# Moving a kernel's stores to another engine's queue, re-anchoring its early loads and shifting one tile in the order

## The chip, the cores and the metric

The kernel runs on one core of one Trainium2 chip. The metric is the device time of one execution in microseconds, as the median of several executions. Before the change it was 1954.47 us (three runs, 1954.44 to 1956.24). One us is 0.05% of the whole.

## The reference

The kernel computes a block and all its gradients: a layer norm, a branch A (a shift convolution over four steps, then a long convolution through an FFT) and a branch B (an MLP with a ReLU gate).

```python
def _A_ref(q, k, v, shift_k, ssm_k, ssm_D):        # S = 2048, D = 1024
    k_shift = sum(k_pad[:, t:t + S, :] * shift_k[:, ks - 1 - t] for t in range(4))
    kv = k_shift * v
    y = irfft2(rfft2(pad(kv)) * rfft2(pad(ssm_k)))[:S] + kv * ssm_D
    return q * y
def _B_ref(x, W_gate, W_up, W_down):               # F = 3584
    gate = x @ W_gate
    return (relu(gate) * (x @ W_up)) @ W_down
xn  = layernorm(x)
out = x + _A_ref(xn, k, v, ...) + _B_ref(xn, ...)
# returned: out and, by jax.vjp, the gradients of all inputs      [abridged]
```

## The kernel before

TensorE works through the MLP in blocks of 512 hidden columns. The A branch is a generator: it handles 128 channels (a *group*) at a time, eight groups in all, and its small matmuls are dealt out between the MLP's. Each engine works through its instructions in the order in which the program was built: a scheduler places each instruction by its priority and by the time at which it expects its inputs.

Loads and nearly all stores go out from SyncE, in one queue:

```python
    def load(self, out, in_):                       # A branch
        self.pri.now()
        ins = self.nc.sync.dma_start(out=out, in_=in_)
        if self.pin:
            self.tc.keep_in_program_order(ins)

    def store(self, out, in_):                      # A branch
        self.pri.late()
        self.nc.sync.dma_start(out=out, in_=in_)
```

The pieces of one group that the argument needs (the group's order of steps, cut):

```python
    def h_tile(self, st):                           # the filter tile
        hT = self.ttile("hT")
        pst = self.ps.tile([P, 16, P], BF16, name="pst", tag="aps")   # PSUM, 2 buffers for the A branch
        for r in range(16):
            self.nc.tensor.transpose(pst[:, r, :], hv[:, r, :], self.identA[:])
        self.vcopy(hT[:, 0:16, :], pst[:])          # VectorE; frees the PSUM buffer
        return hT

    def steps(self):
        self.shift_rows()                           # ends in the store of sk_d
        self.pin = True
        nx = self.loads_1(0)                        # hn, gt, xt, sD
        self.loads_2(nx)                            # kp, vt, skb
        self.pin = False
        hT = self.h_tile(nx)
        for gi in range(self.NG):
            ...
            self.taps(st, ksh, kp, ...)             # 4 products and 3 sums on VectorE, 128 x 2048
            self.tt(kvt[:, 0:16, :], ksh[:], vt[:], ALU.mult)
            ...                                     # nx = loads_1(gi + 1)
            gks = self.gradients(st, gkv, ksh)      # stores gv
            self.store_time(self.y_d, cg, yt)
            self.grad_k(st, gks)                    # stores gk
            self.loads_2(nx)
            ...
            hT = self.h_tile(nx)                    # next group's filter
            yield from self.inv_b_chan(Ch, ghn, 2000)   # two groups of matmuls, ps5, each into an A PSUM buffer
            self.store(self.out_gh[cg, :], ghf)
```

In a group, `gv`, `y`, `gk`, `gt`, `xt`, `kp` and `vt` move between a [2048, 1024] matrix and [128, 16, 128] tiles, in halves of 1024 rows of 256 bytes. The MLP stores `h_d` and `ug_d` for the weight gradients later, and its weights are loaded two blocks deep: `wg`, `wu` as plain loads and `wdT` as four DMA transposes. The early loads are tied to a store:

```python
                        stored = nc.sync.dma_start(out=h_d[...], in_=ht[:])
                        self.stored = stored
    ...
                        with self.tc.issue_after(self.stored.ins):
                            load(5 + sp // 2)                       # layer-norm input
    ...
                        with self.tc.issue_after(self.stored.ins):
                            first = self.weights(Wg, Wu, Wd, fb + 1)
```

Of the kernel before, what the change touches and what calls it, by code (L numbers as in the profile page):

```python
# [17 lines left out]
P = 128  # L18
# [24 lines left out]
class ABranch:  # L43
# [41 lines left out]

    def store(self, out, in_):
        self.pri.late()
        self.nc.sync.dma_start(out=out, in_=in_)

    def open(self):  # L90
        R = "right"
# [333 lines left out]
    def steps(self):  # L425
# [4 lines left out]
        nx = self.loads_1(0)  # L430
        self.loads_2(nx)
        self.pin = False
        hT = self.h_tile(nx)
        for gi in range(self.NG):
            st, nx = nx, None
# [94 lines left out]
class LnMlp:  # L530
# [126 lines left out]

    def load_T(self, src, st, name):
        t = self.act_tile(name)
        self.nc.sync.dma_start_transpose(out=t[:].rearrange("p (a b) -> p a b", b=P),  # L660
                                         in_=src[st * P:(st + 1) * P, :])
        return t

    def flip_xn(self, st):
# [7 lines left out]
    def hidden(self, first, goT, load, ln, tables, Wg, Wu, Wd, g, xn_d, h_d, ug_d):  # L672

        nc, HS = self.nc, self.ST // 2
        for half in range(2):
            s0 = half * HS
# [3 lines left out]
            for fb in range(self.FB):  # L680
                self.pri.now()
                cols = slice(fb * 512, fb * 512 + 512)
                wg, wu, wd = first or self.weights(Wg, Wu, Wd, fb)
                first = None
                ru, ahead = {}, fb + half == 0
# [7 lines left out]
                def gate_up(sp):  # L693
                    flip(sp + 2)
                    for s in (sp, sp + 1):
                        ru[s] = self.e2_tile("ru")
                        ps = self.ps_tile("ps_g")
                        self.gemm8(ps, xT[s], wg)
                        nc.scalar.activation(out=ru[s][:, 0, :], in_=ps[:], func=ACT.Relu)
                        yield 1730  # L700
                        self.pri.now()
                    for s in (sp, sp + 1):
                        ps = self.ps_tile("ps_u")
                        self.gemm8(ps, xT[s], wu)
                        ht = self.e1_tile("ht")
                        nc.vector.scalar_tensor_tensor(out=ru[s][:, 1, :], in0=ru[s][:, 0, :], scalar=0.0, in1=ps[:],  # L706
                                                       op0=ALU.is_gt, op1=ALU.mult)
                        nc.vector.tensor_tensor(out=ht[:], in0=ru[s][:, 0, :], in1=ru[s][:, 1, :], op=ALU.mult)
                        stored = nc.sync.dma_start(out=h_d[(s0 + s) * P:(s0 + s + 1) * P, cols], in_=ht[:])
                        self.stored = stored  # L710
                        yield 1730
                        self.pri.now()

                def grad(sp):
                    for s in (sp, sp + 1):
                        if ahead and s == sp + 1:
                            flip(min(sp + 6, HS))
                        ps = self.ps_tile("ps_h")
                        self.gemm8(ps, gT[s], wd)
                        gh = self.e1_tile("gh")  # L720
                        nc.scalar.copy(out=gh[:], in_=ps[:])  # L721
                        nc.vector.tensor_tensor(out=ru[s][:], in0=ru[s][:], in1=gh[:].rearrange(
                            "p (o f) -> p o f", o=1).to_broadcast([P, 2, 512]), op=ALU.mult)
                        nc.sync.dma_start(out=ug_d[(s0 + s) * P:(s0 + s + 1) * P, :, cols], in_=ru[s][:])
                        yield 1730
                        self.pri.now()

# [7 lines left out]
                for sp in range(0, HS, 2):  # L735
                    self.pri.now()
                    while len(gT) < min(sp + (6 if ahead else 2), HS):
                        gT.append(self.load_T(g, s0 + len(gT), "goT"))
                    if not ahead:
                        yield from gate_up(sp)  # L740
                    yield from grad(sp)
                    if ahead and sp + 4 < HS:
                        with self.tc.issue_after(self.stored.ins):
                            load(5 + sp // 2)
                        yield from gate_up(sp + 4)
                        next(ln)
                    if ahead and sp == 0:
                        with self.tc.issue_after(self.stored.ins):
                            first = self.weights(Wg, Wu, Wd, fb + 1)
                if ahead:  # L750
                    with self.tc.issue_after(self.ln_act.ins), self.tc.issue_after(self.ln_dve.ins):
# [27 lines left out]
    def grad_down(self, g, h_d, out_wd):  # L779
        nc = self.nc  # L780
        self.pri.now()
        gn = self.nat_tiles(g, "g_nat")
        for fb in range(self.FB):
            self.pri.now()
            hs = self.slab(h_d, fb, "hs")
            if fb == 0:
                self.pri.now()
                ps = [self.ps_tile("ps_d") for _ in range(4)]
                wo = [self.e2_tile("wo") for _ in range(2)]
# [9 lines left out]
                        yield 1730  # L799
                        self.pri.now()  # L800
                for j in range(2):
                    nc.sync.dma_start(out=out_wd[j * P:(j + 1) * P, :], in_=wo[j][:].rearrange("p a f -> p (a f)"))
            for j in range(2 if fb == 0 else 0, 4):
                self.pri.now()
                wo = self.e2_tile("wo")
# [3 lines left out]
                                           lambda st: gn[st][:, ob * 512:ob * 512 + 512])  # L809
                    nc.scalar.copy(out=wo[:, ob, :], in_=ps[:])  # L810
                f0 = fb * 512 + j * P
                nc.sync.dma_start(out=out_wd[f0:f0 + P, :], in_=wo[:].rearrange("p a f -> p (a f)"))

    def grad_in(self, xn_d, ug_d, out_wg, out_wu):
        nc = self.nc
# [2 lines left out]
        for fb in range(self.FB):  # L818
            for w, out in ((1, out_wg), (0, out_wu)):
                self.pri.now()  # L820
                sl = self.slab(ug_d[:, w, :], fb, "ugs")
                for dp in range(self.DT // 2):
                    self.pri.now()
                    wo = self.e2_tile("wi")
                    for d in range(2):
# [1 line left out]
                        ps = self.ps_tile("ps_w")  # L827
                        yield from self.gemm16(ps, lambda st: xn[st][:, dc * P:(dc + 1) * P], sl)
                        nc.scalar.copy(out=wo[:, d, :], in_=ps[:])  # L829
                    nc.sync.dma_start(out=out[dp * 256:dp * 256 + 256, fb * 512:fb * 512 + 512].rearrange(  # L830
                        "(s p) f -> p s f", p=P), in_=wo[:])

    def open_right(self, Wd):
# [209 lines left out]
```

## Time and profile before

| | before |
|---|---|
| median of the runs | 1954.5 us |
| TensorE busy, of the profiled span of 1957.4 us | 1915.1 us |
| TensorE idle | 42.3 us, 12.5 of it the first layer norm |
| mean granted TensorE clock (1 is full speed) | 0.995 |
| VectorE waiting for gv stores | 15.9 us |

The profiled run itself took 1959.14 us, more than any of the timed ones. The view of TensorE's waits names, for each group of its instructions, what ended the idle time before it: engine and line of the waiting instruction, "<-", the releaser, then us in total, times, longest. The prediction below shows it whole, with the queue of SyncE.

### The profile page before, as it was taken

The numbers are of one execution on the slowest core, as the hardware profiler recorded it, in microseconds if no ns is written. First come the engines' busy times: TensorE is split into PE (matmuls) and PEld (weight loads), VectorE is DVE, ScalarE is ACT, GpSimd is POOL, SyncE is SP. The second block draws the span as 40 slices with busy tenths as digits, with TensorE's granted clock in tenths as the row PEclk, the third lists the DMA queues.
The fourth block names the chain that finished last, engine by engine and source line by source line (L and its number), as shares of the span: only waits on it lengthen the run. The fifth ranks groups of instructions, "written<-read, shape, count | busy, mean of one in ns | idle before, by whom it ended". The sixth has DMA issues, their size and how long they took to land.

```text
span 1957.4 us, 36111 instructions
## 1 busy us (share of the span) xinstructions
PE 1915.1 (98%) x15502; PEld 882.0 (45%) x15502; DVE 914.1 (47%) x1374; ACT 616.8 (32%) x852; POOL 14.7 (1%) x37
## 2 busy tenths in 40 slices
PE   7899999999999999999999999999999999999998
PEld 3434444444444444444444444444444444444443
DVE  6677677577678557355255435300222222222222
ACT  6544354444444425444344354311000000000000
POOL 1000000000000000000000000000000000000000
PEclk9999999999999999999999999999999999999999
DMA  9975766984674774462763542691999954545441
GB/s 255 237 157 163 178 179 174 207 202 136 168 193 130 202 213 136 113 185 78 224 158 119 127 135 85 159 324 39 239 255 235 210 135 121 123 120 124 123 121 38
DMA packets 615970, 319.08 MB, mean 163 GB/s; under 512 B 450937, under 2 KB 585089, under 8 KB 615809
## 3 DMA queue, kind: packets, MB, share of 16 engines
q1 hardware_dynamic: 605312, 295.79, 60.2%
q10 hardware_dynamic: 9216, 16.78, 2.8%
q0 software_dynamic: 1280, 4.20, 0.8%
q8 instruction: 121, 1.98, 0.4%
q14 instruction: 41, 0.33, 0.1%
HBM read 141.56 MB, written 95.44 MB: 121 GB/s over the span
## 4 chain that ended last, share of the span: by engine, by line
PE 90%; DVE 4%; DMA 3%; issue 2%; ACT 1%; SPq 0%; POOL 0%; DVEq 0%; ACTq 0%; POOLq 0%
PE ps_w L774 20%; PE ps_x L908 19%; PE ps_o L874 10%; PE ps_g L643 9%; PE ps_u L643 9%; PE ps_d L774 8%; PE ps_h L643 8%; PE ps L66 6%; DMA ln_x<-in_A_q_dram 1%; PE ps_d L794 1%; DVE flp L304 1%; ACT ln_j L597 1%; DMA kp<-in_A_k_dram 1%; DVE gk L74 0%; DVE ru L706 0%
## 5 line engine op out<-in xcount | busy, mean ns | idle before, releaser
L774 PE MATMUL ps_w<-ugs,xn_nat 128*128 128x512 bf16 x1792 | 399.4, 379 | 2.1 <-DMA xn_nat<-xn_d 1.3
L643 PEld LDWEIGHTS <-xnT 128*128 128x128 bf16 x1792 | 172.2, 99 | 218.3 <-issue 19.6
L774 PEld LDWEIGHTS <-xn_nat 128*128 128x128 bf16 x1792 | 170.3, 98 | 208.6 <-issue 5.9
L643 PE MATMUL ps_u<-wu,xnT 128*128 128x512 bf16 x896 | 209.4, 384 | 4.7 <-DMA wu<-in_B_W_up_dram 4.1
L643 PE MATMUL ps_g<-wg,xnT 128*128 128x512 bf16 x896 | 209.0, 383 | 2.2 <-DVE xnT L669 2.2
L643 PE MATMUL ps_h<-wdT,goT 128*128 128x512 bf16 x896 | 206.7, 379 | 0.6 <-DMA wdT<-in_B_W_down_dram 0.6
L921 ACT ACTIVATE w<-xn,m 128x512 f32<-128x512 bf16 x32 | 24.3, 806 | 559.5 <-issue 317.2
L908 PE MATMUL ps_x<-wgT,ggT 128*128 128x512 bf16 x896 | 198.6, 379 | 0.0
L908 PE MATMUL ps_x<-wuT,guT 128*128 128x512 bf16 x896 | 198.6, 379 | 0.0
L874 PE MATMUL ps_o<-wd,hT 128*128 128x512 bf16 x896 | 193.6, 379 | 0.0
L774 PE MATMUL ps_d<-g_nat,hs 128*128 128x512 bf16 x832 | 187.4, 379 | 0.0
L304 DVE STREAM_TRANSPOSE flp<-C 128x1024 f32<-128x1024 f32 x48 | 90.4, 1934 | 102.8 <-ACT C L70 102.8
L829 ACT CAST wi<-ps_w 128x512 bf16<-128x512 f32 x112 | 65.6, 587 | 222.4 <-PE ps_w L774 207.9
L908 PEld LDWEIGHTS <-ggT 128*128 128x128 bf16 x896 | 87.7, 98 | 105.7
L908 PEld LDWEIGHTS <-guT 128*128 128x128 bf16 x896 | 87.7, 98 | 105.7
L874 PEld LDWEIGHTS <-hT 128*128 128x128 bf16 x896 | 87.7, 98 | 105.7
L643 PEld LDWEIGHTS <-goT 128*128 128x128 bf16 x896 | 85.1, 98 | 103.5 <-issue 4.5
L304 DVE STREAM_TRANSPOSE flp<-B 128x1024 f32<-128x1024 f32 x48 | 90.4, 1940 | 83.3 <-ACT B L70 83.2
L910 DVE CUSTOM_DVE_ANT_0 gx<-ps_x,gy 128x512 f32<-128x512 f32 x32 | 22.1, 691 | 216.5 <-PE ps_x L908 216.5
L774 PEld LDWEIGHTS <-hs 128*128 128x128 bf16 x832 | 78.5, 98 | 95.5 <-issue 4.3
L721 ACT CAST gh<-ps_h 128x512 bf16<-128x512 f32 x112 | 65.2, 585 | 165.7 <-PE ps_h L643 153.7
L867 DVE TENSOR_TENSOR ya<-ya,xe 128x1024 bf16<-128x1024 bf16 x16 | 11.1, 692 | 226.9 <-DMA xe<-xn_d 226.9
(165 smaller groups left out, 1541.6 us busy)
## 6 DMA issues: line engine op xcount, KB each, us to landing
ug_d<-ru SPq DMA_DIRECT2D x112, 256.0 KB, 3.5
ugs<-ug_d SPq DMA_DIRECT2D x112, 256.0 KB, 4.6
wg<-in_B_W_gate_dram SPq DMA_DIRECT2D x56, 256.0 KB, 4.2
wu<-in_B_W_up_dram SPq DMA_DIRECT2D x56, 256.0 KB, 3.4
h_d<-ht SPq DMA_DIRECT2D x112, 128.0 KB, 2.4
hs<-h_d SPq DMA_DIRECT2D x56, 256.0 KB, 4.7
out_dram<-wi SPq DMA_DIRECT2D x56, 256.0 KB, 3.1
gt<-in_grad_out_dram SPq DMA_DIRECT2D x32, 256.0 KB, 3.4
```

The source lines that it names most:

```text
L66: self.nc.tensor.matmul(out, lhsT=lhsT, rhs=rhs, start=start, stop=stop)
L304: self.nc.vector.transpose(out=df[:, c0:c0 + 32, :], in_=sf[:, c0:c0 + 32, :])
L597: total = nc.scalar.activation(out=jk[:], in_=xt[:, j, :], func=ACT.Copy, accum_out=sm[:, 0, j:j + 1])
L643: self.nc.tensor.matmul(ps[:], lhsT=xT[:, kt * P:(kt + 1) * P], rhs=w(kt), start=(kt == 0), stop=(kt == self.DT - 1))
L721: nc.scalar.copy(out=gh[:], in_=ps[:])
L774: self.nc.tensor.matmul(ps[:], lhsT=lhsT(st), rhs=rhs(st), start=(st == 0), stop=(st == self.ST - 1))
L794: nc.tensor.matmul(ps[i][:], lhsT=hs(st)[:, j * P:(j + 1) * P], rhs=gn[st][:, ob * 512:ob * 512 + 512], start=(st == 0), stop=(st == self. ...
L829: nc.scalar.copy(out=wo[:, d, :], in_=ps[:])
L874: nc.tensor.matmul(ps[:], lhsT=hT[:, kt, :], rhs=self.wd[:, kt, oc], start=(kt == 0), stop=(kt == self.FT - 1))
L908: nc.tensor.matmul(ps[:], lhsT=T[:, kt, :], rhs=W[:, kt, oc], start=(i == 0), stop=(i == n - 1))
L910: V.tensor_tensor_reduce(out=gx[:, oc], in0=ps[:], in1=gy[:, oc], scale=1.0, scalar=0.0, op0=ALU.add, op1=ALU.add, accum_out=m[:, ob:ob + 1])
L921: nc.scalar.activation(out=w[:, oc], in_=xn[:, oc], func=ACT.Identity, scale=m[:, 5:6], bias=m[:, 4:5])
```

## The change

The intent: SyncE's queue is in order, and loads stand in it behind stores that wait for VectorE. All stores up to the weight gradients move to GpSimd, so that SyncE holds loads only in that part; the early loads are anchored on a transpose load instead of a store; and the first filter tile is made some steps later than its load.

```diff
     def store(self, out, in_):
         self.pri.late()
-        self.nc.sync.dma_start(out=out, in_=in_)
+        self.nc.gpsimd.dma_start(out=out, in_=in_)
@@ steps
         self.pin = False
+        yield 8000
         hT = self.h_tile(nx)
@@ load_T
-        self.nc.sync.dma_start_transpose(out=..., in_=src[st * P:(st + 1) * P, :])
+        self.loaded = self.nc.sync.dma_start_transpose(out=..., in_=src[st * P:(st + 1) * P, :])
@@ hidden
-                        stored = nc.sync.dma_start(out=h_d[...], in_=ht[:])
-                        self.stored = stored
+                        nc.gpsimd.dma_start(out=h_d[...], in_=ht[:])
@@ hidden
-                        nc.sync.dma_start(out=ug_d[...], in_=ru[s][:])
+                        nc.gpsimd.dma_start(out=ug_d[...], in_=ru[s][:])
@@ hidden, twice
-                        with self.tc.issue_after(self.stored.ins):
+                        with self.tc.issue_after(self.loaded.ins):
@@ weight gradients, three places (out_wd twice; out_wg and out_wu)
-                nc.sync.dma_start(out=out_wd[...], in_=wo...)
+                nc.gpsimd.dma_start(out=out_wd[...], in_=wo...)
```

(Index expressions are cut.)

More of the change, by code (lines that the diff above doesn't have):

```diff
@@ L659, in load_T @@
         t = self.act_tile(name)
-        self.nc.sync.dma_start_transpose(out=t[:].rearrange("p (a b) -> p a b", b=P),
-                                         in_=src[st * P:(st + 1) * P, :])
+        self.loaded = self.nc.sync.dma_start_transpose(out=t[:].rearrange("p (a b) -> p a b", b=P),
+                                                       in_=src[st * P:(st + 1) * P, :])
         return t
@@ L708, in gate_up @@
                         nc.vector.tensor_tensor(out=ht[:], in0=ru[s][:, 0, :], in1=ru[s][:, 1, :], op=ALU.mult)
-                        stored = nc.sync.dma_start(out=h_d[(s0 + s) * P:(s0 + s + 1) * P, cols], in_=ht[:])
-                        self.stored = stored
+                        nc.gpsimd.dma_start(out=h_d[(s0 + s) * P:(s0 + s + 1) * P, cols], in_=ht[:])
                         yield 1730
@@ L723, in grad @@
                             "p (o f) -> p o f", o=1).to_broadcast([P, 2, 512]), op=ALU.mult)
-                        nc.sync.dma_start(out=ug_d[(s0 + s) * P:(s0 + s + 1) * P, :, cols], in_=ru[s][:])
+                        nc.gpsimd.dma_start(out=ug_d[(s0 + s) * P:(s0 + s + 1) * P, :, cols], in_=ru[s][:])
                         yield 1730
@@ L747, in hidden @@
                     if ahead and sp == 0:
-                        with self.tc.issue_after(self.stored.ins):
+                        with self.tc.issue_after(self.loaded.ins):
                             first = self.weights(Wg, Wu, Wd, fb + 1)
@@ L801, in grad_down @@
                 for j in range(2):
-                    nc.sync.dma_start(out=out_wd[j * P:(j + 1) * P, :], in_=wo[j][:].rearrange("p a f -> p (a f)"))
+                    nc.gpsimd.dma_start(out=out_wd[j * P:(j + 1) * P, :], in_=wo[j][:].rearrange("p a f -> p (a f)"))
             for j in range(2 if fb == 0 else 0, 4):
@@ L811, in grad_down @@
                 f0 = fb * 512 + j * P
-                nc.sync.dma_start(out=out_wd[f0:f0 + P, :], in_=wo[:].rearrange("p a f -> p (a f)"))
+                nc.gpsimd.dma_start(out=out_wd[f0:f0 + P, :], in_=wo[:].rearrange("p a f -> p (a f)"))
     def grad_in(self, xn_d, ug_d, out_wg, out_wu):
@@ L829, in grad_in @@
                         nc.scalar.copy(out=wo[:, d, :], in_=ps[:])
-                    nc.sync.dma_start(out=out[dp * 256:dp * 256 + 256, fb * 512:fb * 512 + 512].rearrange(
+                    nc.gpsimd.dma_start(out=out[dp * 256:dp * 256 + 256, fb * 512:fb * 512 + 512].rearrange(
                         "(s p) f -> p s f", p=P), in_=wo[:])
```

## The prediction

> **What bounds the kernel now.** I read the engine summary first, then who TensorE waited for, then the clock by slices of 5 us, then the queue that issues the transfers. The page opens with:
>
> ```profile
> PE 1915.1 (98%) x15502; PEld 882.0 (45%) x15502; DVE 914.1 (47%) x1374; ACT 616.8 (32%) x852; POOL 14.7 (1%) x37
> ```
>
> TensorE (PE) is busy for 1915.1 of 1957.4 us. The change touches no matmul, so all that it can win is the 42.3 us in which PE is idle, plus time that PE spends at a reduced clock. The view of PE's waits over the whole span splits the idle time (columns: engine, line, what ended the wait, us in total, times, longest):
>
> ```profile
> PE pst_x L667 <- DVE ln_b L609: 10.4, 1, 10.4
> PE ps L66 <- DVE hT L78: 6.1, 4, 2.5
> PE pst L293 <- DMA hn<-in_A_ssm_k_dram: 4.5, 1, 4.5
> PE ps_u L643 <- DMA wu<-in_B_W_up_dram: 4.1, 1, 4.1
> PE ps_g L643 <- DVE xnT L669: 2.2, 2, 1.1
> PE pst_x L667 <- DVE ln_x L624: 2.1, 1, 2.1
> PE ps L66 <- DVE flp L304: 1.7, 3, 0.9
> PE ps_w L774 <- DMA xn_nat<-xn_d: 1.3, 3, 0.7
> PE ps_w L774 <- DMA out_dram<-wo: 0.7, 1, 0.7
> PE ps_h L643 <- DMA wdT<-in_B_W_down_dram: 0.6, 1, 0.6
> PE ps_u L643 <- ACT gh L721: 0.5, 1, 0.5
> ```
>
> The eleven lines sum to 34.2 us. The first and the sixth (12.5 us) are the first layer norm, before PE has anything to do; the rest of the 42.3 us, 8.1, is mostly the drain after the last matmul. That leaves 34.2 - 12.5 = 21.7 us of waits which the order of transfers could touch, and only two of them are loads of some size: hn, the first filter tile, 4.5, and wu, a block of the up weights, 4.1. After 960 us the view shows no wait of PE.
>
> The slices of 5 us show what each pause costs afterwards (columns: stretch, its length, busy time of PE, PEld, DVE, ACT and POOL with instruction counts, granted clock, DMA share, GB/s):
>
> ```profile
> 90.00:95.00 5.00, 0.76 (x8) 0.77 (x9) 0.95 (x2) 0.00 (x0) 0.00 (x0) 0.82 1.16 227
> 95.00:100.00 5.00, 5.00 (x21) 2.43 (x20) 1.22 (x1) 0.00 (x0) 0.00 (x0) 0.50 1.35 166
> 125.00:130.00 5.00, 3.34 (x9) 1.21 (x9) 4.90 (x5) 0.00 (x0) 0.00 (x0) 0.73 1.11 238
> ```
>
> After the hn wait the clock is 0.50 for a whole slice, after the wu wait 0.73. At (1 - clock) x 5 us these are 0.9 + 2.5 and 1.35 us, and the slice 130 to 135 (clock 0.93) adds 0.35.
>
> Why those two loads are late is in the timeline of the issuing queue (start, length, queue, line, what, how many):
>
> ```profile
> 87.94 0.56 SPq L88 DMA_DIRECT2D sk_d<-sk_t  x1
> 88.59 0.54 SPq L724 DMA_DIRECT2D ug_d<-ru  x1
> 89.19 0.60 SPq L82 DMA_DIRECT2D hn<-in_A_ssm_k_dram  x1
> ...
> 111.70 5.34 SPq L709 DMA_DIRECT2D h_d<-ht  x2
> 119.08 2.92 SPq L724 DMA_DIRECT2D ug_d<-ru  x2
> 122.09 3.01 SPq L636 DMA_DIRECT2D wu<-in_B_W_up_dram  x4
> ```
>
> The queue is in order. The hn load goes out at 89.19 behind stores of ug_d, and PE reaches it half a us later; wu goes out at 122.09 behind stores of h_d and ug_d that wait for a VectorE which is busy throughout 115 to 130 us. Both are waits behind stores, not a lack of bandwidth: the DMA share from 110 to 120 is 0.08 to 0.10.
>
> **What the Trainium skill says.** "DMA: Bandwidth & Descriptors", section "Issuing engines are not separate DMA queues", says that transfers issued from several engines share the same 16 DMA engines and that spreading them only saves issue time. I read it as: no bandwidth to win, only the wait in order; the DMA shares above agree. The same page, "Latency and other measured facts", gives about 1 us to the first byte from GpSimd against about 0.6 from SyncE. In this trace the 16 xn_d stores from GpSimd land in a median of 6.0 us and stores of the same 256 KB from SyncE in 2.1 to 4.4, though the former all fall in the crowded first 80 us. "SBUF — State Buffer", section "SBUF: two separate sides", warns that VectorE operations in its two-port modes lock GpSimd out of writing descriptors. The trace shows little of it: the xn_d issues take 539 ns at the median and 682 at most beside a VectorE that is 46% to 83% busy in those slices. "TensorE: Matmul & The Clock Gate", Part 1, puts the clock at one half after about 3.4 us of idleness, and full again after about 3.4 busy us; the 0.50 slice after a 4.5 us wait agrees.
>
> **The change part by part.** (1) 112 h_d, 112 ug_d, 28 wo and 56 wi stores, the 48 halves of gv, y and gk, 8 ghn and 3 small ones, 367 in all, move from SyncE to GpSimd. At 0.54 us (xn_d) that is 198 us of GpSimd issue time spread over 1270 us, on an engine busy 14.7 us: off the path. The 48 halves have rows of 256 bytes, 1024 of them against 128 for xn_d; if issue time scaled with rows they would cost 8 x 0.54 = 4.3 us each (estimate), together 207 instead of 26 us. The engine would still be under a third busy.
>
> (2) SyncE's rows fall from 1016 to some 650. In the order of the changed kernel hn is queued directly after the last layer-norm load, behind no store; that load went out at 49.0 us before, so hn should be in the buffer some 25 us before PE asks. xt, kp and vt follow at about 75 to 85 instead of 91.6 to 101. The wu block, the third, takes the buffers of the second block's gate tiles, whose last matmuls in the timeline run from 105.04 to 108.7. Before it SyncE's new order has only loads whose waits end sooner. So it can go out at about 109 and, at the 3.4 us of the wu issues, land at about 113, ten us before PE wants it at 122.5.
>
> (3) The 8000 ns step moves the filter transpose in PE's order. Counting matmul time at 2.4 GHz, it stands 3.5 us later (74.4 against 71.0 us of PE work), and all of the A branch follows 8 to 9 us later. It lies inside the MLP's matmuls, and 97 us of matmuls without any A work follow its end, so the shift costs nothing by itself.
>
> (4) The layer-norm and weight loads now hang on a transpose load instead of on a store: earlier, in a stretch where the DMA share is already about 1. A risk of one or two us.
>
> Sum: hn 4.5 + 0.9 + 2.5 = 7.9; wu 4.1 + 1.35 + 0.35 = 5.8; together 13.7. I keep 80%, 11, since PE arriving sooner can meet VectorE (busy 4.9 of 5 us around 125) instead. The hT waits, 6.1 us, hang on VectorE's in-order work; VectorE itself waited 15.9 us for gv stores and 7.3 for kp loads, which the change moves both ways. I take 1 us off for these. The small loads (xn_nat, wdT: 1.9) give perhaps 1, and I set 2 us against the sum for new waits. Net 11 + 1 + 1 - 2 = 11 us: 1954.5 - 11 = 1943.5.
>
> **The rivals.** *The wait is only replaced.* VectorE fell behind at 115 to 130 because tap work arrives together with MLP work. With loads earlier this work starts earlier, which speaks against it; but if PE then waits for flp, kvt or PSUM banks, the gain shrinks to 3 to 5 us: 1950.
>
> *GpSimd stores land so late that buffers bind.* The A branch has three time tiles for hT, kvt, gv, gks, yt, gk and ghn, each freed by a store. Against 4.4 us now, 10 us of landing would add 5 to 6 us to VectorE's wait in each of 8 groups. Also the zeroing of kp sits in GpSimd's queue behind stores. If a third of 8 x 6 us reached PE, +16 us would cancel the gain: 1955 to 1960. For it: 6.0 us of xn_d, and the row counts. Against: PE has other matmuls in its order between dependent A steps, and the gv stores today are themselves held up on SyncE.
>
> *More is won.* If all 21.7 us of waits and all clock loss went (mean clock 0.995, so 0.005 x 1957 = 9.8 us, 0.8 of it after the last matmul) the win would be 30.7 us, 1.6%. So over 2% (39.1 us) is out of reach unless the start also shortens, for which I see nothing.
>
> **Range and chances.** Centre 1943.5. The low end, 1934, takes both loads in full and most of hT with its clock loss; the high end, 1955, is the buffer rival cancelling everything. Faster by 2% needs below 1915.4: 1 in 100. Slower by 2% needs above 1993.6, some 50 us of new waits, only if descriptor making is far slower than xn_d shows: 3 in 100. Same: 96 in 100.
>
> **What would show it.** Right: the waits on hn and wu are absent, the clock stays at 1.00 from 85 to 135, PE's busy time falls by about 4 us and its idle time by 7 or more; the hn issue starts before 65 us; the stretch after 1369 is unchanged. Wrong: waits of PE on hT, flp or ps banks that grow beyond 10 us in sum, VectorE waiting for gv, gk or y stores well above 20 us, or GpSimd's store issues of several us each. An early wait on ln_x, were it to grow, would refute step (4).

## The result

The changed kernel takes 1971.14 us in the median (four runs, 1968.44 to 1972.56), the kernel before 1954.45 us on the same chip (four runs, 1952.49 to 1956.24). Ratios here and below are the mean time of one kernel's fast runs over that of the other's fast runs of the same rounds, so not quite the ratio of the medians: here 1.0084, 95% interval 1.0066 to 1.0101. That is 0.8% slower, the same at a threshold of 2%. The prediction said 1943.5 with a range of 1934 to 1955, so it missed, and in sign.

The engine summary of the changed kernel:

```profile
PE 1917.8 (97%) x15502; PEld 882.5 (45%) x15502; DVE 914.6 (46%) x1374; ACT 618.4 (31%) x852; POOL 255.6 (13%) x404
```

GpSimd (POOL) is at 13%, no bound. TensorE's idle time rose from 42.3 to 52.4 us of a span of 1970.2. Its waits:

```profile
PE ps L66 <- DVE hT L78: 11.5, 6, 3.0
...
PE ps_h L644 <- DMA wdT<-in_B_W_down_dram: 10.0, 6, 3.3
PE ps L66 <- DVE flp L304: 4.1, 2, 3.6
...
PE ps_w L774 <- DMA xn_nat<-xn_d: 1.9, 4, 1.3
PE ps_g L644 <- DVE ru L707: 1.9, 3, 1.3
```

Set this against the same view of before in the prediction. The waits on hn (4.5) and on wu (4.1) are gone, as predicted. In their place wdT went from 0.6 to 10.0, hT from 6.1 to 11.5, flp from 1.7 to 4.1. The wdT waits fall into two stretches, at 69 to 76 and at 415 to 422 us. The slices of 5 us (stretch, length, busy time of PE, PEld, DVE, ACT, POOL, clock, DMA share, GB/s) show the second:

```profile
415.00:420.00 5.00, 1.06 (x5) 0.29 (x4) 1.09 (x2) 1.01 (x1) 0.54 (x1) 1.00 1.19 243
420.00:425.00 5.00, 4.04 (x10) 1.28 (x10) 0.69 (x1) 0.59 (x1) 0.00 (x0) 0.51 1.09 315
425.00:430.00 5.00, 5.00 (x20) 2.11 (x19) 0.69 (x1) 2.27 (x4) 1.35 (x2) 0.80 0.19 65
```

TensorE lost 3.94 + 0.96 = 4.9 us, and the clock of 0.51 and 0.80 took 0.49 x 5 + 0.20 x 5 = 3.5 more. At 70 to 85 us the same reading gives 5.1 and, with clocks of 0.54 and 0.78, 3.4. A sum over the changes: the wdT waits with their clock, 8.4 + 8.5 = 16.9, less the 0.6 of before; hT and flp +7.8; ru and xn_nat, 1.9 + 0.6 = +2.5; hn and wu, -13.7 by the prediction's count. That is +12.9, against 12.8 between the two profiled spans (that it agrees to a tenth is chance). The profiled runs took 1971.92 and 1959.14 us; the medians lie 16.7 us apart, so some 4 us of the loss are outside this sum.

The queue of SyncE (start, length, queue, line, what, how many) ahead of the second stretch:

```profile
385.93 0.36 SPq L82 DMA_DIRECT2D skb<-sk_d  x1
397.97 0.60 SPq L82 DMA_DIRECT2D xt<-xn_d  x1
398.67 1.00 SPq L82 DMA_DIRECT2D hn<-in_A_ssm_k_dram  x1
399.76 2.56 SPq L637 DMA_DIRECT2D wu<-in_B_W_up_dram  x4
402.37 0.98 SPq L82 DMA_DIRECT2D xt<-xn_d  x1
403.45 16.07 SPq L652 DMA_TRANSPOSE wdT<-in_B_W_down_dram  x4
```

SyncE stands for 12 us, and the next in its queue is xt, whose pool is shared with VectorE's taps (e7 below tests whether that buffer is the reason). Then two halves of xt, hn and wu, 2 MB together, go out within 5.4 us, and the four wdT transposes take 16 us behind them. In the kernel before they went out one by one between stores, and wdT cost TensorE 0.6 us in the whole run:

```profile
408.32 1.26 SPq L651 DMA_TRANSPOSE wdT<-in_B_W_down_dram  x1
...
410.31 1.25 SPq L651 DMA_TRANSPOSE wdT<-in_B_W_down_dram  x1
...
412.26 2.57 SPq L651 DMA_TRANSPOSE wdT<-in_B_W_down_dram  x2
```

And one of the six hT waits, first on VectorE, then on TensorE (columns as above; in brackets the idle time before and what ended it):

```profile
242.84 2.47 DVE L74 TENSOR_TENSOR ksh<-ksh,tap 128x2048 bf16<-128x2048 bf16 x2
245.23 1.22 DVE L74 TENSOR_TENSOR tap<-kp,skb 128x2048 bf16<-128x2048 bf16 x1
246.37 1.22 DVE L78 COPY hT<-pst 128x2048 bf16<-128x2048 bf16 x1
247.50 1.21 DVE L74 TENSOR_TENSOR ksh<-ksh,tap 128x2048 bf16<-128x2048 bf16 x1
```

```profile
239.56 1.16 PE L293 MATMUL pst<-ident,hn 128*128 128x128 bf16 x16
...
242.29 0.63 PE L66 MATMUL ps<-RB,flp 128*128 128x64 bf16 x16
242.75 1.89 PE L644 MATMUL ps_u<-wu,xnT 128*128 128x512 bf16 x8
247.64 0.63 PE L66 MATMUL ps<-RB,flp 128*128 128x64 bf16 x16 [2.99 <-DVE hT L78]
```

TensorE had made pst, the transposed filter, by 240.72. VectorE copies it at 246.37, because the next group's taps (ksh, tap) stand in front of the copy. Until then pst keeps one of the A branch's two PSUM buffers, and the second ps5 group of matmuls (247.64) has nowhere to go. The order of the built program shows this for every group. Counted are the tap operations (4 products, 3 sums) of a group that stand on VectorE before the copy of that same group's hT:

```
                      group  0  1  2  3  4  5  6  7    sum
kernel before                0  1  2  3  4  5  2  3     20
changed kernel               1  6  6  6  7  6  6  6     44
```

The stores themselves, which I had feared, are not late: gv's halves land in 4.6 us instead of 4.4, y's in 4.7 instead of 4.3, gk's in 5.1 instead of 4.4 (medians of those landings that the traces show, 5 to 8 of 16 before and 9 to 14 after). They also go out sooner: between a tile being ready and its store going out lay a median of 7.3 us for gv, 14.3 for y and 13.7 for ghn before, and 0.3 to 1.1 us after (worked out from the two traces).

### The profile page after: what moved, and what is told of

Read it like the earlier page. It is cut to its first block, busy times and chain, and to the rows that moved or that the text cites. A ratio compares the mean times of both kernels' runs of the same rounds, so it can differ in the third digit from the quotient of the medians.

```text
span 1970.2 us, 36231 instructions
## 1 busy us (share of the span) xinstructions
PE 1917.8 (97%) x15502; PEld 882.5 (45%) x15502; DVE 914.6 (46%) x1374; ACT 618.4 (31%) x852; POOL 255.6 (13%) x404
## 3 DMA queue, kind: packets, MB, share of 16 engines
q0 software_dynamic: 27424, 87.07, 14.3%
## 4 chain that ended last, share of the span: by engine, by line
PE 89%; DVE 5%; issue 2%; DMA 2%; ACT 1%; SPq 0%; POOL 0%; DVEq 0%; ACTq 0%; POOLq 0%
PE ps_w L774 19%; PE ps_x L908 19%; PE ps_o L874 10%; PE ps_h L644 9%; PE ps_g L644 9%; PE ps_u L644 9%; PE ps_d L774 9%; PE ps L66 6%; DVE tap L74 1%; DVE flp L304 1%; DMA wdT<-in_B_W_down_dram 1%; DVE ksh L74 1%; DMA xn_nat<-xn_d 1%; DMA kp<-in_A_k_dram 0%; DVE gk L74 0%
## 5 line engine op out<-in xcount | busy, mean ns | idle before, releaser
L644 PE MATMUL ps_h<-wdT,goT 128*128 128x512 bf16 x896 | 211.2, 386 | 10.0 <-DMA wdT<-in_B_W_down_dram 10.0
L304 DVE STREAM_TRANSPOSE flp<-C 128x1024 f32<-128x1024 f32 x48 | 90.7, 1940 | 107.0 <-ACT C L70 107.0
L707 DVE SCALAR_TENSOR_TENSOR ru<-ru,ps_u 128x512 bf16<-128x512 bf16 x112 | 76.4, 682 | 80.3 <-PE ps_u L644 37.7
```

The lines of the kernel that those rows point to most:

```text
L304: self.nc.vector.transpose(out=df[:, c0:c0 + 32, :], in_=sf[:, c0:c0 + 32, :])
L644: self.nc.tensor.matmul(ps[:], lhsT=xT[:, kt * P:(kt + 1) * P], rhs=w(kt), start=(kt == 0), stop=(kt == self.DT - 1))
L707: nc.vector.scalar_tensor_tensor(out=ru[s][:, 1, :], in0=ru[s][:, 0, :], scalar=0.0, in1=ps[:], op0=ALU.is_gt, op1=ALU.mult)
```

## The experiments

There were three theories.

- **G**: GpSimd's stores free buffers too late, and the copy of hT waits for its tile.
- **W**: with no stores on SyncE, the A branch's loads stand in front of the weights there.
- **O**: the stores' move changed the static order of VectorE; the copy of hT now stands behind the next group's taps.

Two more, **P** and the case of xt, arose on the way. All eighteen runs gave correct results. "Before" in each is from the same chip and rounds; its median lay between 1955.1 and 1956.3. Edits are against the changed kernel unless said otherwise.

### First round: e1 to e4

**e1** holds the first A loads behind the second block's last wdT transpose.

```diff
-        nx = self.loads_1(0)
-        self.loads_2(nx)
+        with self.tc.issue_after(self.mlp.turned.ins):   # turned: the last wdT transpose issued
+            nx = self.loads_1(0)
+            self.loads_2(nx)
```

> The changed kernel, with the A branch's first loads (hn, gt and the rest) issued behind the second block's weight transposes instead of ahead of them. Theory W (A loads in front of weights on SyncE): PE's three waits on wdT at 69 to 76 us (5.1 us) and the clock loss after them (about 3.4 us) go, so about 8 us faster than the changed kernel, some 1963; the wdT waits at 415 to 422 stay. Theory G (stores from GpSimd land later and buffers bind): little change in that stretch's successors, the total stays within 3 us of 1971.

Measured: 1967.63 us (1965.62 to 1970.99), ratio to before 1.0063 [1.0047, 1.0079]. The first stretch of wdT waits is gone (wdT 4.7 in all), but at 65 to 70 us TensorE now waits 3.2 us for ScalarE's gh. hT stays at 11.8. So the early jump of the A loads is worth some 3 us, not the loss, and less than the 8 that W had expected.

**e2** puts the A branch's 59 stores back on SyncE; MLP and weight-gradient stores stay on GpSimd. **e3** does the opposite for h_d and ug_d.

```diff
 e2, in store:      -  self.nc.gpsimd.dma_start(out=out, in_=in_)
                    +  self.nc.sync.dma_start(out=out, in_=in_)
 e3, in hidden:     -  nc.gpsimd.dma_start(out=h_d[...] / ug_d[...], ...)
                    +  nc.sync.dma_start(out=h_d[...] / ug_d[...], ...)
```

> The changed kernel with the A branch's stores (gv, y, gk, ghn, small ones) back on SyncE, all other stores on GpSimd. In the built order the first hn load falls back behind the second block's weights. Theory W: both groups of wdT waits shrink below 2 us in sum, 1955 to 1960. Theory G: VectorE's wait on gv stores falls from 33.6 towards 16 us and the hT waits from 11.5 towards 6; the time falls by as much, 5 us, to about 1966, and wdT waits stay.

> The changed kernel with h_d and ug_d stores back on SyncE (224 of 367), the A branch's and the weight gradients' stores on GpSimd. Theory W: with SyncE full again the A loads fall behind weights as before, wdT waits under 1 us, 1953 to 1958. Theory G: gv waits of VectorE stay near 33 us and hT waits near 11, so 1960 to 1966.

Measured: e2 1949.06 (1944.29 to 1952.64), ratio 0.9965 [0.9945, 0.9985], so faster than before; e3 1965.87 (1964.7 to 1967.44), 1.0053 [1.0038, 1.0068]. The whole loss hangs on the A branch's stores, although they are 59 of 367. hT waits: 6.8 in e2, 10.1 in e3. Taps before hT, counted as above: 33 in e2, 41 in e3.

**e4** takes away what G says the hT step waits for: gv is written over ksh, so no time tile is held by a gv store.

```diff
-        gv = self.ttile("gv")
-        self.tt(gv[:, 0:16, :], gkv[:, 0:16, :], ksh[:], ALU.mult)
-        self.store_time(self.out_gv, cg, gv)
+        self.tt(ksh[:], gkv[:, 0:16, :], ksh[:], ALU.mult)
+        self.store_time(self.out_gv, cg, ksh)
```

> The changed kernel with gv written over ksh, so that gv takes none of the three time tiles and gk no longer waits for the gv store. Theory G: VectorE's 33.6 us of waits on the gv store go, hT waits fall from 11.5 us to 6 or less, total 5 to 8 us faster, about 1964. Theory W: less than 3 us, the wdT waits (10 us) stay.

Measured: 1966.02 (1961.11 to 1969.47), ratio 1.0059 [1.0039, 1.0078]. VectorE's waits for gv stores fell from 33.6 us to none, and TensorE's hT wait was 13.2, against 11.5 in the changed kernel. G is refuted for the hT step as far as gv goes: it was not a late gv store that held it.

### Second round: the order of VectorE alone

**e5** adds one order to the changed kernel: a group's taps come behind the copy of its hT. No store or load changes its queue, and no buffer changes.

```diff
 h_tile:
-        self.vcopy(hT[:, 0:16, :], pst[:])
+        self.pri.late()
+        self.hT_copied = self.nc.vector.tensor_copy(out=hT[:, 0:16, :], in_=pst[:])
 steps:
-            self.taps(st, ksh, kp, [(3, 0), (2, 1), (1, 2), (0, 3)])
+            with self.tc.issue_after(self.hT_copied.ins):
+                self.taps(st, ksh, kp, [(3, 0), (2, 1), (1, 2), (0, 3)])
```

> The changed kernel with one order added on VectorE: the shift taps of a group come behind the copy of that group's hT. Nothing is removed and no store or load moves queue. Theory O (the longer hT and flp waits come from VectorE's static order: the next group's taps, whose loads now come early, stand before the copy that frees the PSUM bank): PE's wait on hT falls from 11.5 (13.2 in e4) to under 4 us, flp with it to under 2, and the time falls by 5 to 9 us from 1966 to 1971, to 1960 to 1964. Rival (the copy waits for its time tile or for a store, or the ps5 group waits for PSUM whatever the order): hT stays over 8 us and the time within 3 us. The wdT waits, about 10 us, should stay in both.

Measured: 1946.18 (1940.86 to 1954.91), ratio to before 0.9964 [0.9935, 0.9992]. That is 25 us less than the changed kernel. In the built programs, TensorE's order differs from the changed kernel's in the place of two matmuls, ScalarE's in nothing; of VectorE's 1374 instructions 48 stand elsewhere, of SyncE's 652 transfers 11. The same place in e5's trace, VectorE and TensorE:

```profile
237.37 1.22 DVE L295 COPY hT<-pst 128x2048 bf16<-128x2048 bf16 x1 [1.37 <-PE pst L293]
238.51 1.22 DVE L74 TENSOR_TENSOR ksh<-kp,skb 128x2048 bf16<-128x2048 bf16 x1
```

```profile
238.90 0.63 PE L66 MATMUL ps<-RB,flp 128*128 128x64 bf16 x16
239.36 1.89 PE L646 MATMUL ps_u<-wu,xnT 128*128 128x512 bf16 x8
241.09 0.63 PE L66 MATMUL ps<-RB,flp 128*128 128x64 bf16 x16
```

The copy follows pst at once, the same eight matmuls lie between the two ps5 groups, and the second waits for nothing. hT and flp are gone from the view of waits. O had expected 5 to 9 us, and that the wdT waits of 10 us would stay; it got 25, and wdT fell to 1.3. So e5 changed more than the hT step: VectorE's taps hold xt's buffers, too. SyncE in e5, where the changed kernel stood for 12 us:

```profile
390.40 2.94 SPq L639 DMA_DIRECT2D wu<-in_B_W_up_dram  x4
394.32 6.55 SPq L654 DMA_TRANSPOSE wdT<-in_B_W_down_dram  x4
400.97 1.33 SPq L82 DMA_DIRECT2D xt<-xn_d  x2
```

With the taps later, the scheduler puts xt behind the transposes. They take 6.6 us instead of 16.1, and the wait at 415 to 422 is gone. How much of the 25 us is the hT step alone and how much is xt's place on SyncE, no run separates. Aligning each trace's weight loads by the matmul work ahead of them shows where the two kernels part (us behind the kernel before; negative is ahead; profiled runs):

```
before's time      221    289    380    453    612    748    936    end
changed kernel    -5.0   -0.8   -1.5   +5.3   +9.1   +8.5  +14.0  +12.9
e5                -6.9   -7.3   -8.0  -11.5  -11.1  -17.0  -15.9  -18.4
```

The changed kernel was ahead at 221 us, by the hn and wu waits that it does save. It gives this back, and more, by 936 us, in four steps of 4 to 7 us.

**e6** takes away the shift of the first filter tile (the line `yield 8000`).

> The changed kernel without the shift of the first filter tile by 8000 ns of steps. My prediction took the shift for free. If so: within 3 us of the changed kernel, 1966 to 1971, with wdT and hT waits alike. Rival (the shift lines A-group ends up badly with the MLP work and makes part of the loss): 5 us or more faster.

Measured: 1974.72 (1970.7 to 1980.52), ratio 1.0097 [1.0074, 1.012], beside 1.0084 with the shift: it is no faster without the shift, so no harm from it shows.

**e7** gives the pool of xt and taps a third buffer (`self.pool("a_tmp", 3, side=R)`).

> The changed kernel with three buffers instead of two in the pool of xt and the taps. Theory W, second part (SyncE stands about 12 us at 386 to 398 us for xt's buffer with the third block's wu and wdT loads behind it, and PE then waits 4.9 us for wdT at 415 to 422): SyncE's stand before that xt shrinks below 4 us, the wdT wait at 415 to 422 is gone, wdT in all about 5 us, and the time falls by 4 to 7 us to 1960 to 1966. Rival (those transposes are slow for another reason, single ones taking up to 6.6 us): the wait stays. VectorE's order around hT is the same as in the changed kernel, so hT stays at 10 to 13 us.

Measured: 1963.64 (1963.01 to 1973.39), ratio 1.005 [1.0023, 1.0076]. SyncE's stand before xt fell from 12 to 5.5 us (expected: under 4), the transposes of the third block took 8.8 us, and the time fell by about the expected 4 to 7 us. But the first stretch of wdT waits is gone too, which this buffer was not expected to touch, so not all of it belongs to the second. hT is at 15.2, above the 10 to 13 expected: the hT waits don't hang on this buffer.

**e8** is e2 with e5's order.

> e2 (A-branch stores on SyncE, all others on GpSimd) with e5's order of VectorE. e2 ran at 1949.06 with 6.8 us of hT waits. Theory O: hT under 3 us and 1943 to 1947. Rival: hT replaced by another wait (flp, kvt), 1948 to 1951.

Measured: 1940.45 (1937.56 to 1942.45), ratio 0.9919 [0.9902, 0.9935]. The hT waits of e2 (6.8) are gone, as O says, and the time is below the 1943 to 1947 that O expected.

### Third round: what the change is worth when the order is held

**e9** is the kernel *before* with e5's order; **e10** and **e11** are e5 and e8 again; **e12** is the kernel *before* with nothing but the new anchor.

```diff
 e12, against the kernel before:
-        self.nc.sync.dma_start_transpose(...)
+        self.loaded = self.nc.sync.dma_start_transpose(...)
-                        with self.tc.issue_after(self.stored.ins):      # twice
+                        with self.tc.issue_after(self.loaded.ins):
```

> The kernel before with e5's one order on VectorE (taps of a group behind the copy of its hT), all stores still on SyncE. This tells what the change itself is worth once the order is held: e5 against this run. If the order is a defect of both kernels, this run gains about the hT and flp waits of before (6.1 + 1.7 us) and some clock, 1945 to 1950, and the change adds nothing or little. If the order is a defect that the change brings in, this run stays within 3 us of before, 1952 to 1957, and the change with the order held (e5) wins 8 to 12 us over it, as my prediction summed.

> e5 once more with five rounds, since its four runs scattered from 1940.9 to 1954.9: expected 1940 to 1948, ratio to before 0.993 to 0.997.

> e8 once more with five rounds, beside e10 on the same chip. If the A-branch's stores on GpSimd cost nothing by themselves and only through the order that they let arise, e10 and this run are within 3 us; if they also cost by themselves (landing, buffers), e10 is 4 us or more slower. Expected 1939 to 1943.

> The kernel before with only the fourth part of the change: the early loads of layer norm and weights hang on a transpose load instead of on a store of h_d. My prediction gave it a risk of one or two us. If so 1953 to 1958. Rival (the anchor alone brings the weights in front of the A loads or takes away the wu wait): 1948 to 1952; or it crowds the first 80 us: over 1958.

Measured, five rounds each: e9 1950.0 (1949.41 to 1953.66), ratio 0.9975 [0.9962, 0.9989]; e10 1948.18 (1942.91 to 1956.18), 0.9966 [0.9945, 0.9988]; e11 1940.72 (1937.53 to 1944.02), 0.9926 [0.991, 0.9941]; e12 1951.66 (1946.07 to 1952.24), 0.998 [0.9966, 0.9994].

Now the loss can be split, roughly: e10's runs scatter over 13 us. Holding the order gains 5.1 us in the kernel before (1955.1 to 1950.0) and 23.0 in the changed one (1971.1 to 1948.2, on different chips). With the order held on both sides, the change is worth 1948.2 - 1950.0 = -1.8 us, which is not clear of zero (the intervals of the two ratios overlap almost wholly). So the 17 us by which the changed kernel is slower are gone once VectorE's order is held on both sides, together with what that order moves on SyncE. The anchor alone wins 3 us; the prediction had feared it would cost one or two. In e12's trace hn goes out at 84.74 instead of 89.19, its wait is 1.3 us instead of 4.5, and the clock stays at 1.00 in the slices after it. The count of taps ahead of hT is 20 in e12 and 39 in e6, so neither the anchor nor the shift brings the order about; the moved stores do.

But the whole change with the order held (e10) is still 7.5 us behind the one without the A branch's stores (e11). That was left open.

### Fourth round: e13 to e16

W says that A loads block the weights on SyncE. A new theory, **P**, says that the A branch's stores and loads compete with the weights for the DMA engines, and that one in-order queue had kept them apart.

**e13** is e10 with the A branch's loads on GpSimd, too. **e14**, **e15** and **e16** are e10 with gk's stores, with gv's and y's, and with all three back on SyncE.

```diff
 e13, in load:     -  ins = self.nc.sync.dma_start(out=out, in_=in_)
                   +  ins = self.nc.gpsimd.dma_start(out=out, in_=in_)
 e14, in grad_k:   +  self.store_time(self.out_gk, st["cg"], gk, self.nc.sync)
 e15:              +  self.store_time(self.out_gv, cg, gv, self.nc.sync)
                   +  self.store_time(self.y_d, cg, yt, self.nc.sync)
 e16:                 the three lines of e14 and e15
```

> e10 (the changed kernel with hT first) with the A-branch's loads issued from GpSimd too, so that they queue behind that branch's stores again and SyncE holds weights, layer norm and gradients only. W (A loads stand in front of the weights on SyncE): PE's waits on wdT, hs and g_nat go and the time falls from 1948 to 1938 to 1943. P (the stores compete with the loads whatever the queue of the A loads): 1945 to 1952, waits on wdT, hs or g_nat stay. If loads of 512 KB issued from GpSimd come too late for the filter and taps, slower than 1952 with PE waits on hn or DVE waits on kp.

> e10 with the gk stores alone back on SyncE. S for gk (its stores fall into the crowded hand-over from one MLP block to the next): most of the 7 us come back, 1940 to 1944. If gk is one of several: 1944 to 1948.

> e10 with the gv and y stores back on SyncE, gk on GpSimd. S for gk: no gain, 1946 to 1950. S for gv or y: 1940 to 1944.

> e10 with gv, y and gk stores back on SyncE; ghn and the small store of sk_d, which in e11 too were on SyncE, stay on GpSimd. If the time-form stores make the 7 us: 1937 to 1941, at or below e11, since the early part up to 220 us was 3 us ahead in e10. If ghn or sk_d matter: 1944 to 1948.

Measured: e13 1971.88 (1961.08 to 1977.54), ratio 1.0084 [1.0059, 1.0108]; e14 1940.12 (1935.72 to 1949.28), 0.9929 [0.991, 0.9949]; e15 1938.98 (1936.6 to 1941.68), 0.9917 [0.9904, 0.9929]; e16 1939.23 (1937.06 to 1940.93), 0.9917 [0.9904, 0.993].

e13 refutes W. SyncE held no A load, and the wait for wdT rose to 17.2 us, most of it in one stretch (waits from 380 to 450 us, then SyncE, then GpSimd):

```profile
PE ps_h L646 <- DMA wdT<-in_B_W_down_dram: 11.6, 3, 6.9
```

```profile
394.42 16.46 SPq L654 DMA_TRANSPOSE wdT<-in_B_W_down_dram  x4
```

```profile
396.63 0.86 POOL L82 DMA_DIRECT2D xt<-xn_d  x1 [0.78 <-DVE ru L709]
402.94 1.09 POOL L82 DMA_DIRECT2D xt<-xn_d  x1
```

The transposes went out when e10's did (394.4 against 395.8) and took 16.5 us instead of 6.2, with two xt loads beside them. e14 is the cleanest run on the stores themselves. In the built programs just the 16 gk stores change their queue; the orders of TensorE, VectorE and ScalarE are e10's. Still the median falls from 1948.2 to 1940.1, by the ratios 0.4%, though the two intervals touch. So a store on GpSimd can cost without any change of order. e14 and e15 have the same median as e16: no single store is the culprit, and moving part of them back is enough (e14's runs still scatter over 14 us, as e10's do over 13; those of e15 and e16 over 4 to 5). e10 itself shows how close it runs: the profiled run of e5 (1940.86) has wdT waits of 1.3 us, that of the same program in e10 (1953.1) has 4.9, and 5.2 more for hs and g_nat at 695 to 706 us, with clocks of 0.77 and 0.55.

"DMA: Bandwidth & Descriptors" in the Trainium skill fits this in two sections. "SWDGE vs HWDGE vs iDMA" says that GpSimd's and SyncE's transfers feed different internal queues of each DMA engine, and that the engine takes turns between them. So a store moved to GpSimd no longer queues behind a load; it takes its share beside it. No run here shows the turns, only what would follow from them. "Why small descriptors are slow (HBM only)" puts the overhead of 256-byte descriptors at 27%. The A branch's halves have such rows, and in the changed kernel 256 KB of gv land in 4.6 us, 512 KB of ghn, whose rows have 4 KB, in 4.1. That is further apart than 27%, but the two go out at different places of the program, so it doesn't test the figure.

### Fifth round: is it xt beside the transposes?

In the runs so far, the four transposes took 15 to 16.5 us where both halves of xt went out beside them or in the six us before (the changed kernel, e1, e4, e13), 7.1 to 8.8 with one half just before (e2, e3, e7) and 5.5 to 8.5 where xt stood behind (e5, e8, e10, e11, e14 to e16). That is only read off. **e17** takes xt out of the way in e13, **e18** puts it beside in e16.

```diff
 e17, against e13:   -  self.load_time(xt, self.xn_d, cg)                     # GpSimd
                     +  self.load_time(xt, self.xn_d, cg, self.nc.sync)
 e18, against e16:   -  self.load_time(xt, self.xn_d, cg)                     # SyncE
                     +  self.load_time(xt, self.xn_d, cg, self.nc.gpsimd)
```

> e13 (1971.9) with xt's loads alone back on SyncE, where they stand behind the block's wdT transposes; all other A loads stay on GpSimd; TensorE's order is the same. If xt's load beside the transposes is the cause: the four transposes of the third block take under 9 us instead of 16.5, PE's 11.6 us of wdT waits at 405 to 425 us are gone, and the time falls by 11 to 16 us to 1955 to 1961. If it is another cause (GpSimd's traffic in general): the transposes stay over 12 us and the time within 5 us of e13.

> e16 (1939.2) with xt's loads alone issued from GpSimd, where they need not stand behind the transposes; TensorE's and ScalarE's orders are the same. If xt beside the transposes is the cause: the four transposes of the third block take 12 us or more instead of 6.2, PE waits for wdT at 405 to 425 us and the time rises by 5 to 15 us to 1944 to 1954. If not: within 3 us of e16.

Measured: e17 1965.01 (1961.89 to 1966.92), ratio 1.0043 [1.0031, 1.0056]; e18 1945.61 (1944.48 to 1946.14), 0.9946 [0.9934, 0.9957].

Both moved in the direction expected. e17 fell short of its size; e18's time is within its range, but its transposes are not, and most of its loss came from elsewhere. In e17 the transposes took 11.7 us instead of 16.5 (SyncE, then GpSimd), and the wdT wait of 380 to 450 us went from 11.6 to 1.8. But with the other A loads still on GpSimd the early part got slower (a new wait of 6.9 us for xnT), and 1965 is above the 1961 I had set.

```profile
401.73 11.67 SPq L654 DMA_TRANSPOSE wdT<-in_B_W_down_dram  x4
```

```profile
397.58 0.83 POOL L82 DMA_DIRECT2D hn<-in_A_ssm_k_dram  x1
```

In e18 the transposes there took 10.2 us instead of 6.2 and cost a wait of just 1.8. Most of its 6.4 us came earlier. In e16, kp's loads stand on SyncE behind xt and go out from 83.42 on. With xt gone from that queue they went out at 52.89 and 69.34, beside the second block's transposes. Those took 11.3 us instead of 6.8, TensorE waited 7.5 us for wdT, and the clock fell to 0.50 and 0.60 in two slices. So xt is one case of it, and in e17 something besides xt kept the transposes at 11.7 us. The traces show a candidate that I had not tested: hn, 512 KB in rows of 4 KB. In e17 it goes out 4.1 us before the first transpose and lands 3.7 us after that one's issue; in e13 and the changed kernel, too, it goes out 4 to 5 us before; in e5, e10, e16 and e18 6.5 us before, and in e16 it has landed by then. No run moves hn alone. What both runs support is that xt's loads beside the weight transposes lengthen them, by 4 to 5 us. That other loads of the A branch (hn, kp) do so, too, is only read off.

| run | what | median us | ratio to before | hT | flp | wdT |
|---|---|---|---|---|---|---|
| changed kernel | | 1971.1 | 1.0084 | 11.5 | 4.1 | 10.0 |
| e6 | without the shift | 1974.7 | 1.0097 | 13.1 | 3.8 | 5.7 |
| e4 | gv over ksh | 1966.0 | 1.0059 | 13.2 | 1.8 | 5.0 |
| e7 | third buffer for xt, taps | 1963.6 | 1.0050 | 15.2 | 1.7 | - |
| e2 | A stores on SyncE | 1949.1 | 0.9965 | 6.8 | 0.8 | - |
| e10 | order held | 1948.2 | 0.9966 | - | - | 4.9 |
| e11 | order held, A stores on SyncE | 1940.7 | 0.9926 | - | - | - |
| e16 | order held, gv, y, gk on SyncE | 1939.2 | 0.9917 | - | - | - |

(The last columns are TensorE's waits in us in the profiled run; "-" is none shown. In the traces of the experiments some matmul records are missing, 238 of 15502 in the first four, so their busy sums aren't compared with those of the two kernels.) e15 and e16 beat both kernels; 16 us, 0.8%, against the kernel before.

## Why the prediction was wrong

**Step 1** (store issue on GpSimd is off the path): right, and its worst case far too high. GpSimd was busy 255.6 us; a half of gv, y or gk took 0.87 us to issue, not the 4.3 I allowed. (SyncE's transfers fell from 1019 to 652 by the traces; I had counted 1016.)

**Step 2** (hn and wu come early): right for these two. hn went out at 47 us, both waits vanished, the clock from 85 to 135 us stayed at 1.00, and the changed kernel was 5 us ahead at 221 us. *This is one step that failed, by what it left out.* It said that SyncE's new order "has only loads whose waits end sooner". Ahead of the third block's wu this held (out at 106.10, predicted 109); I took it for the whole run. Loads wait for their own buffers, and at 386 us SyncE stood 12 us in front of xt. And without stores in the queue the A branch's loads went out together, beside the transposes of wdT, which I had at 0.6 us of waits and which came to 10.0, with 6.9 of clock loss.

**Step 3** (the shift is free): right. e6 without it was no faster.

**Step 4** (the anchor, a risk of one or two us): wrong in sign, small. Alone it won 3 us (e12).

**The hT step**: "I take 1 us off for these." *This is the step whose repair turns the sign (e5, e10).* I had put the hT waits down to VectorE's in-order work, rightly, but took that order as given and looked in it for stores and loads that come late. The order itself changed: hT and flp waits rose from 7.8 to 15.6 us. I had the order of the built program at hand and read from it SyncE and TensorE only; counting the taps ahead of hT would have shown 44 instead of 20. Held right, that order, with what it moves on SyncE, is worth 23 us in the changed kernel and 5 in the one before.

**The rivals**: "The wait is only replaced" is what happened, with waits other than those I named apart from flp. "GpSimd stores land so late that buffers bind" was the nearest in us (1955 to 1960, measured 1971), for a reason that e4 and the landing times speak against. The stop signs I had set, hT and flp over 10 us and gv waits well above 20 (33.6), did show, though gv's waits cost TensorE nothing: e4 took them away and won at most 5 us. Right again: the time after 1369 us did not change, and "over 2%" was out of reach.

With the order held, e5 and e10 come to 1946 and 1948, within my range. That would have been luck: the kernel before falls to 1950.0 with the same order (e9), so the change itself is then worth some 2 us, and not the 11 of my sum. By these runs the rest is lost to the moved A stores: with gv, y and gk back on SyncE (e16) the ratio is 0.9917 beside e9's 0.9975, which is some 11 us.

**Left open.** Why gk alone or gv with y are each enough (e14, e15). Whether it is the rows of 256 bytes or the number of bytes that slows the transposes; no run separates them. Whether it was hn that kept the transposes at 11.7 us in e17, with no xt beside them. How the 23 us of the held order divide between the hT step and xt's place on SyncE. And why the first 80 us, with a DMA share around 1.1, show the wdT wait in some profiles and a wait for gh in others.

## What to carry to other kernels

When a scheduler sets a static order, a change to one queue can change the order of every engine: compare the built orders of all engines before predicting, and look at what stands in front of each copy that frees a PSUM buffer. In this kernel the in-order queue that mixes loads and stores was also a brake: it held back bulk traffic that nobody was waiting for, and without it that traffic went beside the transfers that TensorE does wait for (e13, e14, e18). So try moving the stores that loads really stand behind (here the MLP's) without those of the other branch: with the order held that gave 1940 us (e8, e11).

## What the Trainium skill lacked or had wrong

- "DMA: Bandwidth & Descriptors", section "Issuing engines are not separate DMA queues", says that several issuing engines only save the time it takes to initiate a transfer. Here the choice of queue changed what competed with what: gv, y and gk on GpSimd or on SyncE made 1948.2 or 1939.2 us (e10, e16; ratios 0.9966 and 0.9917), though the medians of their own landing differ by 0.2 to 0.8 us only. In e14 the queue of gk's stores was all that changed. The section could say that one in-order queue also decides which transfers run side by side.
- The same page, section "DMA Transpose (X-bar)", has nothing on how long a transpose takes beside other loads. Four transposes of 256 KB took 5.5 to 8.5 us to go through SyncE with xt's loads behind them, and 15 to 16.5 us with both halves of xt beside them or just before (11.7 in e17, where xt stood behind them, too).
- The same page, section "Anatomy of one DMA — SWDGE (gpsimd) path", calls the making of descriptors small and variable. The runs give numbers for the whole issue on GpSimd: 0.56 us on average for a store of h_d, 128 rows, and 0.87 us for one of gv, 1024 rows of 256 bytes, so eight times the rows cost 1.6 times the time.
- No page says that moving a transfer to another queue can reorder engines it doesn't touch. Here 44 instead of 20 tap operations came to stand in front of the copies of hT, and holding that order won 23 us in the changed kernel and 5 in the one before.
